# Router logits summed in PSUM on two quarters of the array's columns, in place of four partial rows and summing products

## The chip, the cores and the metric

One core of a Trainium2 chip runs the whole program. The metric is device time in microseconds for one execution; the table below has the median of three runs of the kernel before. Engines are called by their names here and by the profile's short names in the rows: TensorE (PE, its weight loads PEld), VectorE (DVE), ScalarE (ACT), GpSimd (POOL), SyncE (SP, its queue SPq).

## The reference

Two parts follow each other. A retention layer (4 batches, 8 heads, 768 tokens, 64 wide) gives rows x of 512 elements for 3072 tokens. A mixture of 8 experts then sends every token to the expert whose embedding has the largest logit:

```python
xn = x / (np.linalg.norm(x, axis=-1, keepdims=True) + 1e-06)
en = expert_emb / (np.linalg.norm(expert_emb, axis=-1, keepdims=True) + 1e-06)
logits = xn @ en.T / tau
expert_idx = np.argmax(logits, axis=1)
probs = np.exp(logits - logits.max(-1, keepdims=True))
gate_w = (probs / (probs.sum(-1, keepdims=True) + 1e-09))[np.arange(N), expert_idx]
out[mask] = gate_w[mask, None] * (np.maximum(x[mask] @ w1[e], 0.0) @ w2[e])   # for each expert e
```

The change concerns `x @ en.T`, the logits before the row norm, and what is made of them: the difference to the largest one and the choice of the expert.

## The kernel before, in words

The program is one written-out order of instructions for each engine; no scheduler moves them. It has two stages.

**Retention with routing (up to about 112 us).** Twelve blocks `m` of 256 tokens each go through a loop. For a block TensorE does, in this order: the scores of the 256 tokens (`scores`, L398), the products of queries with the state (`inter`, L466), the state of the next block (`state`, L433), the logits of the block before (`logits_products`, L515), four runs of four transposes that turn the keys and queries of the next block (L367, L385), and the products of values with masked scores (`intra`, L466 again). PSUM tiles for scores, logits and turned blocks come from four banks in rotation (`pt_`), so a run of transposes takes the bank that an earlier step of the same block had, once VectorE or ScalarE has read it. Blocks 0 to 2 get their logits only in block 3, all three at once, since the normed expert embedding `enT` is not ready sooner.

The 512 elements of a row lie as four row blocks of 128 in `yTs[m]` (128 partitions x 4 x 256 tokens). `logits_products` makes one product of 256 tokens for each of the four row blocks: its weights are `enT[:, j]` (128 x 32, of which 8 columns are experts), and the four products write the four different quarters of PSUM's partitions, that is of the array's columns. They are partial sums. `logits_rows` (L523) turns them on VectorE, 32 x 32 at a time, to `parts`, with tokens on the partitions. For a group of blocks (`GROUPS`: blocks 0-2, 3-5, 6-7, 8, 9-10, 11) `sums` (L533) then adds the four partial sums by four products with a 0/1 matrix (`quarters`), which also puts four sets of 32 tokens onto the 128 partitions. `choose` (L541 on) takes the maximum and the difference, finds the expert, `add_counts` counts, and in the next block `count` (L563 on, TensorE) and `ranks` give every token its place in its expert's table, to which GpSimd writes it (`place`, L599).

Rows of x go to memory by SyncE's queue (`rows`, L502), after VectorE has turned them (`rows_turn`, L495). From block 8 on SyncE also loads the weights of the experts (L211 to L220). Loads and rows that stand late in that queue carry a dependence on the early gather of tokens for expert 0 (L628).

**Experts (from about 114 us).** For each expert TensorE makes 96 products of the first layer (L265) and 96 or more of the second (L1117, L1163) from operands that are split into a high and a low part; VectorE makes the low part of the weights (L243) and of the hidden layer (L271). Two tiles of high and low columns, `xh`/`xl` and `hh`/`hl`, are views made by `columns` (L1091) with a distance between planes given by `PITCH` (L45).

Of the kernel before, what the change touches and what calls it, by code (L numbers as in the profile page):

```python
# [11 lines left out]
F32 = mybir.dt.float32  # L12
F32R = mybir.dt.float32r
# [4 lines left out]
ALU = mybir.AluOpType  # L18
AX = mybir.AxisListType
# [5 lines left out]
P = 128  # L25
B, H, S, D = 4, 8, 768, 64
T2 = 2 * P
# [14 lines left out]
CAP = max(CAPS)  # L42
NXC = -(-CAP // Q)
CAPW = NXC * Q
PITCH = [CAP if c % P == 0 else c if e == NE - 2 else CAPW for e, c in enumerate(CAPS)]  # L45
OV = 352
EARLY = 280
TURNED = [c % P > 0 and e < NE - 1 for e, c in enumerate(CAPS)]
# [61 lines left out]
def retention_moe(ctx: ExitStack, tc: tile.TileContext, q, k, v, emb, tau, w1, w2, const, const16, out):  # L110
# [401 lines left out]
    def logits_products(m, ps=None):  # L512
        ps = pt_() if ps is None else ps
        for j in range(KT):
            nc.tensor.matmul(ps[j * Q:(j + 1) * Q, :T2], enT[:, j, :], yTs[m][:, j, :], start=True, stop=True,  # L515
                             skip_group_check=True)
        return ps

    def logits_rows(m, ps):
        g = group_of[m]  # L520
        if g not in parts:
            parts[g] = ap_.tile([P, max(map(len, GROUPS)), 2, NQ, Q], F32, name="parts")
        nc.vector.transpose(out=parts[g][:, m - GROUPS[g][0]].rearrange("p u g e -> p (u g) e"),  # L523
                            in_=ps[:, :T2].rearrange("p (g b) -> p g b", b=Q))

    def span(g):
        return slice(2 * GROUPS[g][0], 2 * GROUPS[g][-1] + 2)
# [1 line left out]
    def sums(g, ps=None, fresh=False, room=None):  # L529
        nm = len(GROUPS[g])  # L530
        ps = pt_() if ps is None else ps
        for i in range(NQ):
            nc.tensor.matmul(ps[i * Q:(i + 1) * Q, :2 * nm * NE], C("quarters"),  # L533
                             parts[g][:, :nm, :, i, :NE].rearrange("p m u e -> p (m u) e"), start=not fresh, stop=True,
                             skip_group_check=True)
        at = room if fresh else ps[:, 64:]
        return [a[:, :2 * nm * NE].rearrange("p (n e) -> p n e", e=NE) for a in (ps, at)] + [at[:, 48:48 + NE]]

    chosen = []

    def choose(g, zs):  # L541
        z, w, _ = zs
        r = span(g)
        nb = r.stop - r.start
        bc = lambda t: t.unsqueeze(2).broadcast_to([P, nb, NE])
        m = ap_.tile([P, nb], F32, name="m", bufs=1)
        nc.vector.tensor_reduce(out=m, in_=z, axis=AX.X, op=ALU.max)
        yield
        nc.vector.tensor_tensor(out=z, in0=z, in1=bc(m), op=ALU.subtract)
        yield  # L550
        nc.vector.scalar_tensor_tensor(out=w, in0=z, scalar=0.0,
                                       in1=C("e16").unsqueeze(1).broadcast_to([P, nb, NE]), op0=ALU.is_lt, op1=ALU.add)
        yield
        nc.vector.tensor_reduce(out=wmn[:, r], in_=w, axis=AX.X, op=ALU.min)
        yield
        chosen.append(nc.vector.tensor_tensor(out=oh[:, r], in0=w, in1=bc(wmn[:, r]), op=ALU.is_equal))
        yield
# [253 lines left out]
    for m in range(NM):  # L811
# [57 lines left out]
        else:  # L869
# [28 lines left out]
            if m == 2:  # L898
                after(nc.sync.dma_start(
                    out=tbl.rearrange("(e s) c -> e (s c)", e=NE)[:, :FILL * SW].rearrange("e (p x) -> e p x", p=P // NE),  # L900
                    in_=none), i)
            for i in () if m < 3 else (0, 1, 2) if m == 3 else (m - 1,):
                logits_rows(i, logits_products(i))
            if m == NM - 5:
                pad(0, spare(0, 3), True)
# [4 lines left out]
            if nxt:  # L910
                state_sums(m + 1)
                if m == NM - 2:
                    lows[0]()
                transpose_k(m + 1, 0)
                transpose_q(m + 1, 0)
                i = transpose_q(m + 1, 1)
                if m + 3 < NM:
                    after(load_v(m + 3), i)
                transpose_k(m + 1, 1)
                if done is not None:  # L920
                    z = sums(done, spare(0, done % 3), True, spare(0, 3))
                    run_all(choose(done, z))
                    run_all(add_counts(done, z))
                if m == NM - 2:
                    lows[1]()
                if m == NM - 2:
                    load_piece(gathered)
                    load_piece(gathered)
                rows(m - 1, gathered if m == NM - 2 else None)
                intra(m, 0)  # L930
                intra(m, 1)
            else:
                intra(m, 0)
                take(m, 0)
                rows_turn(m - 1, (0,))
                z = sums(done)
                run_all(choose(done, z))
                run_all(add_counts(done, z))
                rows_turn(m - 1, (1,))
                rows(m - 1, x=xs_[m - 1])  # L940
                intra(m, 1)
# [146 lines left out]

    xts = {}

    def columns(name, k, e):  # L1091
        t = hp.tile([P, k, CAPW], F32R, name=name)
        return t.rearrange("p k c -> p (k c)")[:, :k * PITCH[e]].rearrange("p (k c) -> p k c", k=k)

    def x_turn(e, kt):
        if kt == 0:
            xTs[e] = (columns("xh", KT, e), columns("xl", KT, e))
        xt = xts[e, kt] = mp.tile([P, NXC, Q], F32, name="xt", bufs=2)
        n = blocks_of(e)
        nc.vector.transpose(out=xt[:, :n], in_=xgs[e][:, :n, kt * Q:(kt + 1) * Q])  # L1100
# [176 lines left out]
    for e in range(1, NE):  # L1277
        nxt = e + 1 < NE
        c = CAPS[e]
        cols = slice(0, c)  # L1280
        hh, hl = columns("hh", FT, e), columns("hl", FT, e)
        gsteps = iter(())
        last = None
        for ft in range(FT):
# [166 lines left out]
```

## Time and profile before

| what | value |
|---|---|
| median of 3 runs | 396.85 us (396.44 to 399.21) |
| the profiled execution | 396.12 us |
| its span, first to last instruction | 394.3 us |
| granted TensorE clock over the span | 1.000 |
| TensorE busy | 384.3 us, 97% |
| VectorE, ScalarE, GpSimd busy | 252.6, 214.6, 154.8 us |

The span is the time from the first to the last instruction of one profiled execution; its own time of 396.12 us has 1.8 us around the span. Times inside the span count from its start. "Busy" is time in which at least one instruction of the engine or the group runs, so a group of overlapping products has less busy time than its count times its mean. The chain is followed back from the last instruction, at each step to what released it.

### The profile page before, as it was taken

What the parts mean: (1) busy time and instruction counts of PE and PEld (TensorE: products, weight loads), DVE (VectorE), ACT (ScalarE), POOL (GpSimd) and SP (SyncE); (2) the same over time, 40 slices, a digit from 0 to 9 for tenths busy, and PEclk for the clock granted to TensorE, in tenths of its full rate; (3) what the DMA queues carried; (4) which work ended last, traced back from release to release, by engine and by line L of the source; (5) the groups of instructions that cost most, each with busy time, mean ns of one, the idle gap of its engine ahead of it and who ended that gap; (6) DMA issues with size and microseconds to landing.
All of it is one profiled execution on the core that took longest, in us unless ns stands there. A gap on an engine that the chain in (4) does not pass through costs nothing.

```text
span 394.3 us, 9699 instructions
## 1 busy us (share of the span) xinstructions
PE 384.3 (97%) x3714; PEld 359.4 (91%) x3714; DVE 252.6 (64%) x536; ACT 214.6 (54%) x383; POOL 154.8 (39%) x177
## 2 busy tenths in 40 slices
PE   7999999988999999999999999999999999999995
PEld 3899888877879898999999999999889999999985
DVE  5496876977988648853871874667357756476500
ACT  3585566655876175526553843935675534573411
POOL 2856397585844614203802510530282131121032
PEclk9999999999999999999999999999999999999999
DMA  7898999689469787976778796886979676675121
GB/s 237 260 305 256 268 267 281 180 240 262 98 197 288 237 249 217 298 183 225 251 244 215 257 333 184 256 282 204 264 259 347 191 230 227 169 240 158 30 107 56
DMA packets 91029, 89.20 MB, mean 226 GB/s; under 512 B 10796, under 2 KB 69548, under 8 KB 90972
## 3 DMA queue, kind: packets, MB, share of 16 engines
q1 hardware_dynamic: 85916, 75.39, 64.1%
q0 software_dynamic: 4880, 13.03, 9.2%
q8 instruction: 31, 0.51, 0.6%
q14 instruction: 26, 0.21, 0.2%
q10 hardware_dynamic: 176, 0.07, 0.1%
HBM read 65.00 MB, written 18.79 MB: 212 GB/s over the span
## 4 chain that ended last, share of the span: by engine, by line
PE 77%; DMA 13%; DVE 4%; issue 2%; SPq 1%; POOL 1%; POOLq 0%; ACT 0%; DVEq 0%
DMA out_dram<-og,si 10%; PE b L265 10%; PE pst L1117 9%; PE py L466 9%; PE py L265 8%; PE py L1117 7%; PE pst L265 6%; PE b L398 6%; PE b L1117 4%; PE pst L433 3%; PE pst L1163 3%; PE b L367 3%; PE b L385 2%; PE b L515 2%; PE pst L1203 2%
## 5 line engine op out<-in xcount | busy, mean ns | idle before, releaser
L243 DVE TENSOR_TENSOR wlo<-raw,whi 128x1024 fp32r<-128x1024 f32 x64 | 77.6, 1217 | 15.9 <-ACT whi L239 12.9
L1144 POOL DMA_INDIRECT out_dram<-og,si x26 | 27.0, 1039 | 115.0 <-ACT og L1134 65.2
L239 ACT CAST whi<-raw 128x1024 fp32r<-128x1024 f32 x64 | 66.1, 1044 | 1.3 <-DMA raw<-in_moe_w_dram 1.2
L628 POOL DMA_INDIRECT xr<-xd,gi x24 | 29.3, 1220 | 29.5 <-ACT sq L297 14.9
L265 PE MATMUL b<-xh,whi 128*128 128x360 f32 (+5 forms) x104 | 34.3, 334 | 0.0
L265 PE MATMUL b<-xl,whi 128*128 128x360 f32 (+5 forms) x104 | 34.1, 332 | 0.0
L265 PE MATMUL b<-xh,wlo 128*128 128x360 f32 (+5 forms) x104 | 34.0, 332 | 0.0
L419 DVE TENSOR_TENSOR pm<-b,mask 128x512 f32<-128x512 f32 x48 | 29.8, 683 | 4.8 <-PE b L398 4.5
L1100 DVE STREAM_TRANSPOSE xt<-xg 128x384 f32<-128x384 f32 (+1 forms) x28 | 15.6, 578 | 25.4 <-DMA xg<-xs 25.3
L270 ACT ACTIVATE hh<-b 128x360 fp32r<-128x360 f32 (+5 forms) x26 | 12.6, 484 | 34.9 <-PE b L265 34.9
L356 POOL TENSOR_TENSOR hh<-whi,cst 128x512 f32<-128x512 f32 x22 | 23.1, 1068 | 19.5 <-DVE pm L419 14.3
L599 POOL DMA_INDIRECT tbl<-zt,sloti x24 | 25.4, 1060 | 12.6 <-DVE sloti L590 3.5
L1117 PE MATMUL pst<-hh,wlo 128*128 128x360 f32 (+4 forms) x88 | 29.4, 334 | 0.8 <-DVE wlo L243 0.8
L1117 PE MATMUL pst<-hl,whi 128*128 128x360 f32 (+4 forms) x88 | 29.4, 334 | 0.0
L1117 PE MATMUL pst<-hh,whi 128*128 128x360 f32 (+4 forms) x88 | 29.3, 332 | 0.0
L265 PE MATMUL py<-xl,whi 128*128 128x384 f32 (+5 forms) x84 | 27.7, 334 | 0.0
L265 PE MATMUL py<-xh,whi 128*128 128x384 f32 (+5 forms) x84 | 27.5, 333 | 0.0
L265 PE MATMUL py<-xh,wlo 128*128 128x384 f32 (+5 forms) x84 | 27.2, 330 | 0.0
L361 POOL TENSOR_TENSOR hl<-wlo,cst 128x512 f32<-128x512 f32 x22 | 22.8, 1052 | 10.0 <-DMA wlo<-in_k_dram 8.3
L466 PE MATMUL py<-pm,vs 128*64 128x128 f32 x384 | 24.4, 277 | 1.0 <-issue 1.0
L398 PE MATMUL b<-qT,kT 64*128 64x128 f32 x384 | 24.7, 278 | 0.0
L466 PEld LDWEIGHTS py<-pm,vs 128*64 128x64 f32 x384 | 21.0, 137 | 3.0 <-issue 1.7
(237 smaller groups left out, 1026.0 us busy)
## 6 DMA issues: line engine op xcount, KB each, us to landing
raw<-in_moe_w_dram SPq DMA_DIRECT2D x60, 512.0 KB, 4.7
whi<-in_q_dram SPq DMA_DIRECT2D x24, 256.0 KB, 4.0
xd<-x SPq DMA_DIRECT2D x48, 128.0 KB, 6.3
wlo<-in_k_dram SPq DMA_DIRECT2D x11, 512.0 KB, 6.1
xs<-xr SPq DMA_DIRECT2D x6, 768.0 KB
og<-yt SPq DMA_DIRECT2D x72, 48.0 KB, 3.1
whi<-in_v_dram SPq DMA_DIRECT2D x6, 512.0 KB
wlo<-in_v_dram SPq DMA_DIRECT2D x6, 512.0 KB
```

The source lines that it names most:

```text
L239: nc.scalar.copy(out=views[1], in_=views[0])
L243: nc.vector.tensor_tensor(out=views[2], in0=views[0], in1=views[1].bitcast(F32), op=ALU.subtract)
L265: nc.tensor.matmul(acc[:, :w], a, x[:, kt, cols], start=(n == 0), stop=(n == len(todo) - 1))
L356: return eng.tensor_tensor(out=qs_r[:, m % 3, :, a], in0=qin[m % 3][:, a], in1=w, op=ALU.mult)
L361: return eng.tensor_tensor(out=ks_r[:, m % 3, s, h], in0=kin[m % 3][:, h, s], in1=w[:, h], op=ALU.mult)
L398: nc.tensor.matmul(psc[a][:, j], kTs[m][a * D:(a + 1) * D, j, u].rearrange("p s c -> p (s c)"), q_cols(m, a, j, u), start=True, stop=True, ...
L419: o.append(nc.vector.tensor_tensor(out=pm, in0=psc[a], in1=w, op=ALU.mult))
L466: nc.tensor.matmul(pys[m][u][o * D:(o + 1) * D, j], lhsT, rhs, start=first, stop=True, skip_group_check=True)
L599: i = nc.gpsimd.indirect_dma_start(out=tbl[:, :], out_offset=bass.IndirectOffsetOnAxis(ap=sloti[:, n:n + 1], axis=0), in_=zt[:, n], in_off ...
L628: return nc.gpsimd.indirect_dma_start(out=xr[:n, j, :], out_offset=None, in_=xd[:rows_, :], in_offset=bass.IndirectOffsetOnAxis(ap=gi[:n, ...
L1117: nc.tensor.matmul(acc[:, :c], a[:, f], x[:, kt, :c], start=(n == 0), stop=(n == 3 * FT - 1))
L1144: i = nc.gpsimd.indirect_dma_start(out=out[:, :] if h is None else out.rearrange("t (h x) -> (t h) x", h=2), out_offset=bass.IndirectOffse ...
```

## The change

The logits of a block are summed over the four row blocks in PSUM, by accumulation. The 256 tokens of a block are split into two sets of 128 (`y[:, i::2]`), and each set is accumulated over the four row blocks on a quarter of its own, the first two of the array's columns. A block has eight products of 128 tokens in place of four of 256. VectorE turns the result in two parts of 64 x 64 to `parts`, where the 256 tokens already stand on 128 partitions in two columns. `sums` makes no products any more and only names PSUM space for what follows; `choose` reads the logits from `parts` and puts the maximum into PSUM. The logits of blocks 1 and 2 move behind later transposes of block 3. The planes of the expert tiles get another distance.

```diff
-PITCH = [CAP if c % P == 0 else c if e == NE - 2 else CAPW for e, c in enumerate(CAPS)]
+PITCH = [CAP if c % P == 0 else CAPW for c in CAPS]
     def logits_products(m, ps=None):
         ps = pt_() if ps is None else ps
         for j in range(KT):
-            nc.tensor.matmul(ps[j * Q:(j + 1) * Q, :T2], enT[:, j, :], yTs[m][:, j, :], start=True, stop=True,
-                             skip_group_check=True)
+            y = yTs[m][:, j].rearrange("p (u g b) -> p g u b", u=2, b=Q)
+            for i in range(2):
+                nc.tensor.matmul(ps[i * Q:(i + 1) * Q, :P].rearrange("p (h u b) -> p h u b", h=2, b=Q), enT[:, j, :], y[:, i::2],
+                                 start=(j == 0), stop=(j == KT - 1), skip_group_check=True)
         return ps

     def logits_rows(m, ps):
...
-            parts[g] = ap_.tile([P, max(map(len, GROUPS)), 2, NQ, Q], F32, name="parts")
-        nc.vector.transpose(out=parts[g][:, m - GROUPS[g][0]].rearrange("p u g e -> p (u g) e"),
-                            in_=ps[:, :T2].rearrange("p (g b) -> p g b", b=Q))
+            parts[g] = ap_.tile([P, max(map(len, GROUPS)), 2, Q], F32, name="parts")
+        for h in range(2):
+            nc.vector.transpose(out=parts[g][2 * h * Q:2 * (h + 1) * Q, m - GROUPS[g][0]],
+                                in_=ps[:2 * Q, 2 * h * Q:2 * (h + 1) * Q].rearrange("p (u b) -> p u b", b=Q))

     def sums(g, ps=None, fresh=False, room=None):
         nm = len(GROUPS[g])
         ps = pt_() if ps is None else ps
-        for i in range(NQ):
-            nc.tensor.matmul(ps[i * Q:(i + 1) * Q, :2 * nm * NE], C("quarters"),
-                             parts[g][:, :nm, :, i, :NE].rearrange("p m u e -> p (m u) e"), start=not fresh, stop=True,
-                             skip_group_check=True)
...
     def choose(g, zs):
-        z, w, _ = zs
+        z, w, _, m = zs
...
-        m = ap_.tile([P, nb], F32, name="m", bufs=1)
-        nc.vector.tensor_reduce(out=m, in_=z, axis=AX.X, op=ALU.max)
+        s = parts[g][:, :nb // 2, :, :NE].rearrange("p m u e -> p (m u) e")
+        nc.vector.tensor_reduce(out=m, in_=s, axis=AX.X, op=ALU.max)
         yield
-        nc.vector.tensor_tensor(out=z, in0=z, in1=bc(m), op=ALU.subtract)
+        nc.vector.tensor_tensor(out=z, in0=s, in1=bc(m), op=ALU.subtract)
...
-            for i in () if m < 3 else (0, 1, 2) if m == 3 else (m - 1,):
+            if m > 2:
+                i = 0 if m == 3 else m - 1
                 logits_rows(i, logits_products(i))
...
                 transpose_q(m + 1, 0)
+                if m == 3:
+                    logits_rows(1, logits_products(1))
                 i = transpose_q(m + 1, 1)
...
                 transpose_k(m + 1, 1)
+                if m == 3:
+                    logits_rows(2, logits_products(2))
...
-        hh, hl = columns("hh", FT, e), columns("hl", FT, e)
+        hh = hp.tile([P, FT, CAPW], F32R, name="hh")
+        hl = hp.tile([P, FT, CAPW], F32R, name="hl")
```

TensorE in block 3, before: the logits of blocks 0 to 2 (tiles b_777, b_784, b_790, four products each), the four runs of transposes, the summing products of the first group (`pst_591<-parts`), and the first product of `intra`.

```order
L515 MATMUL b_777<-yT,enT 32x256 x4
L515 MATMUL b_784<-yT,enT 32x256 x4
L515 MATMUL b_790<-yT,enT 32x256 x4
L367 MATMUL b_800<-ident,hl 128x128 x4
L385 MATMUL b_808<-ident,hh 128x128 x4
L385 MATMUL b_814<-ident,hh 128x128 x4
L367 MATMUL b_821<-ident,hl 128x128 x4
L533 MATMUL pst_591<-parts,cst_61 32x48 x4
L466 MATMUL py_698<-pm_710,vs 64x128
```

The same place after: the logits of block 0 (b_777), 1 (b_807) and 2 (b_831), eight products of 128 tokens each.

```order
L517 MATMUL b_777<-yT,enT 32x128 x8
L367 MATMUL b_793<-ident,hl 128x128 x4
L385 MATMUL b_801<-ident,hh 128x128 x4
L517 MATMUL b_807<-yT,enT 32x128 x8
L385 MATMUL b_818<-ident,hh 128x128 x4
L367 MATMUL b_825<-ident,hl 128x128 x4
L517 MATMUL b_831<-yT,enT 32x128 x8
L466 MATMUL py_698<-pm_710,vs 64x128
```

The three sets of logits stand apart, the last one right ahead of `intra`, and the summing products are gone. In the other blocks the logits keep their place ahead of the transposes.

VectorE in block 3, before: it turns the three sets of logits, makes the state sums (`s`), and begins the choice of the first group.

```order
L523 STREAM_TRANSPOSE parts<-b_777 128x256
L523 STREAM_TRANSPOSE parts<-b_784 128x256
L523 STREAM_TRANSPOSE parts<-b_790 128x256
L446 TENSOR_TENSOR s_796<-pst_591,tB 128x256
L451 TENSOR_TENSOR s_798<-pst_591,tB 128x256
L547 TENSOR_REDUCE m<-pst_591 128x6
L549 TENSOR_TENSOR pst_591<-pst_591,m 128x48
```

The same place after.

```order
L526 STREAM_TRANSPOSE parts<-b_777 64x64 x2
L446 TENSOR_TENSOR s_789<-pst_591,tB 128x256
L451 TENSOR_TENSOR s_791<-pst_591,tB 128x256
L526 STREAM_TRANSPOSE parts<-b_807 64x64 x2
L526 STREAM_TRANSPOSE parts<-b_831 64x64 x2
L546 TENSOR_REDUCE pst_591<-parts 128x6
L548 TENSOR_TENSOR pst_591<-parts,pst_591 128x48
```

The state sums now stand ahead of the second and third set, and the maximum and the difference read `parts` itself.

## Rows read from the trace of the kernel before

**Rows 1.** The page: busy time, share of the span, instructions of TensorE.

```profile
PE 384.3 (97%) x3714; PEld 359.4 (91%) x3714; DVE 252.6 (64%) x536; ACT 214.6 (54%) x383; POOL 154.8 (39%) x177
```

**Rows 2.** Stages: start:end, length, busy (count) PE PEld DVE ACT POOL, clock, DMA, GB/s.

```profile
9.00:63.00 54.00, 54.00 (x1119) 48.27 (x1118) 38.96 (x86) 35.66 (x65) 34.17 (x35) 1.00 0.92 272
94.00:112.00 18.00, 18.00 (x325) 15.75 (x323) 16.18 (x41) 14.97 (x24) 14.15 (x18) 1.00 0.55 142
112.00:134.00 22.00, 21.20 (x181) 19.19 (x178) 19.02 (x57) 12.30 (x25) 10.57 (x11) 1.00 0.79 227
160.00:293.00 133.00, 133.00 (x719) 129.77 (x718) 81.30 (x148) 71.54 (x126) 40.27 (x40) 1.00 0.79 243
390.00:394.30 4.30, 0.00 (x0) 0.00 (x0) 0.00 (x0) 0.24 (x1) 0.97 (x1) 1.00 0.10 35
```

**Rows 3.** Waits of TensorE: total us, times, longest.

```profile
PE pst L433 <- issue: 1.2, 1, 1.2
PE py L466 <- issue: 1.0, 1, 1.0
PE pst L1117 <- DVE wlo L243: 0.8, 2, 0.4
```

**Rows 4.** The chain: start us, us, what; logits, transposes and sums.

```profile
38.71 1.43 PE b L515 x24
40.14 0.59 PE b L367 x4
...
41.60 0.44 PE b L367 x4
42.04 0.22 PE pst L533 x8
...
48.36 0.57 PE b L515 x8
```

**Rows 5.** Instructions of L515 and L523 (ns min/median/max), and who waits for L533.

```profile
L515 PE MATMUL b<-yT,enT x96: 379/379/403, 38.6 to 114.3; 128*32 128x256 f32 x96
...
L523 DVE STREAM_TRANSPOSE parts<-b x12: 437/449/450, 39.3 to 114.8; 128x256 f32<-128x256 f32 x12
...
  DVE m L547: 4.6, 6
```

**Rows 6.** The chain: products on two places (x16, x32 of intra), on four (inter).

```profile
42.26 1.90 PE py L466 x32
...
46.41 1.03 PE py L466 x32
...
110.15 1.02 PE py L466 x16
```

**Rows 7.** VectorE in order of time: the maximum of the first group.

```profile
42.33 0.21 DVE L547 TENSOR_REDUCE m<-pst 128x6 f32<-128x48 f32 x1 [1.03 <-PE pst L533]
```

**Rows 8.** Block 5 in order of time, and the lines' row of L495.

```profile
57.31 0.45 DVE L523 STREAM_TRANSPOSE parts<-b 128x256 f32<-128x256 f32 x1 [0.98 <-PE b L515]
...
58.43 0.47 PEld L367 LDWEIGHTS b<-ident,hl 128*128 128x128 f32 x4
...
L495 DVE STREAM_TRANSPOSE x<-yT 128x512 f32<-128x512 f32 x24 | 15.6, 686 | 0.9 <-DMA xd<-x 0.9
```

**Rows 9.** The chain from 101 to 132 us, and a wait of SyncE's queue.

```profile
101.25 0.92 PE pst L433 x32
...
123.00 0.67 DVE x L495
...
132.10 0.89 PE pst L1117 x4
...
SPq L211 <- DMA xge<-xd,gi: 5.7, 1, 5.7
```

**Rows 10.** The chain: 24 first-layer products of experts 5 and 6.

```profile
304.92 3.93 PE b L265 x24
...
324.60 3.94 PE b L265 x24
```

More of the change, by code (lines that the diff above doesn't have):

```diff
@@ L531, in sums @@
         ps = pt_() if ps is None else ps
-        for i in range(NQ):
-            nc.tensor.matmul(ps[i * Q:(i + 1) * Q, :2 * nm * NE], C("quarters"),
-                             parts[g][:, :nm, :, i, :NE].rearrange("p m u e -> p (m u) e"), start=not fresh, stop=True,
-                             skip_group_check=True)
         at = room if fresh else ps[:, 64:]
-        return [a[:, :2 * nm * NE].rearrange("p (n e) -> p n e", e=NE) for a in (ps, at)] + [at[:, 48:48 + NE]]
+        return [a[:, :2 * nm * NE].rearrange("p (n e) -> p n e", e=NE) for a in (ps, at)] + [at[:, 48:48 + NE], at[:, 56:56 + 2 * nm]]
     chosen = []
     def choose(g, zs):
-        z, w, _ = zs
+        z, w, _, m = zs
         r = span(g)
@@ L1089, in retention_moe, with columns @@
     xts = {}
-    def columns(name, k, e):
-        t = hp.tile([P, k, CAPW], F32R, name=name)
-        return t.rearrange("p k c -> p (k c)")[:, :k * PITCH[e]].rearrange("p (k c) -> p k c", k=k)
+    def columns(name, e):
+        t = hp.tile([P, KT, CAPW], F32R, name=name)
+        return t.rearrange("p k c -> p (k c)")[:, :KT * PITCH[e]].rearrange("p (k c) -> p k c", k=KT)
     def x_turn(e, kt):
         if kt == 0:
-            xTs[e] = (columns("xh", KT, e), columns("xl", KT, e))
+            xTs[e] = (columns("xh", e), columns("xl", e))
         xt = xts[e, kt] = mp.tile([P, NXC, Q], F32, name="xt", bufs=2)
```

## The prediction

> **What bounds the kernel now.** I read the summary first [rows 1]: TensorE is busy for 384.3 of the 394.3 us of the span. The stages come second [rows 2]: from 9 to 63 us and from 94 to 112 us TensorE has no idle time at all, and none from 160 to 293 us; the span ends 4.3 us after its last work. The granted clock is 1.00 in each of them, so no part of the time is to be put down to the clock. The waits of TensorE come third [rows 3]: it waits 0.8 us in two places for a low half of the weights from VectorE, and stops twice, for 1.2 and 1.0 us, for nothing that the profile shows. So work added to TensorE in the retention stage (up to 112 us) goes to the end of the run, unless one of these few stops swallows it. Work added to or taken from VectorE, ScalarE and the queues counts only where TensorE waits for it.
>
> The rows of the chain tell what the logits cost TensorE today [rows 4]. The three blocks whose logits are made together (24 instructions, since each product is issued as two) take 1.43 us; a block on its own (8 instructions) takes 0.57 us, and there are nine of those. Sixteen instructions more cost 0.86 us, which is 54 ns each, and 0.14 us is left as a fixed part. One such instruction lasts 379 ns in the records [rows 5], so several run at a time: the four products of a block write four different quarters of the array's columns. The summing products of a group (8 instructions) take 0.22 us.
>
> **The products, part by part.** After the change a block has eight products of 128 columns, 16 instructions, and they use two quarters of the columns only. The columns that pass are as many as before, spread over half the places. The trace has a near relative: the products of values and masked scores inside a block (128 columns, K of 128, two halves of the columns in turn, also two instructions each). 16 of them take 1.02 us and 32 take 1.90 us [rows 6], which is 55 ns for each further one and 0.14 us fixed. I take 1.02 us for a block. That is 0.45 us more than now, for nine blocks 4.05 us. For the three blocks it is 3 x 1.02 - 1.43 = 1.63 us. There the products now stand apart, between transposes (the order of TensorE is in the section on the change): a run of four transposes that follows the logits takes 0.59 us and a later one 0.44 us [rows 4], so one more such passage adds 0.15 us. Sum of what is added: 5.83 us.
>
> The bounds of this term: products on four places at a time (the products of queries and state, 32 in 1.03 us) would make 16 take 0.52 us; products with no overlap at all, such as the full transposes at 0.11 us each (four in 0.44), would make them take 1.76 us. The first would be 0.05 us less for a block than now, the second 1.19 us more. I take the middle one because it has the same K, the same number of columns and the same two places in turn.
>
> The Trainium skill (TensorEngine Tiling (Array Packing), Theoretical Speedup and When to Use Tiling) speaks against this change: a stationary side of at most 32 columns lets four column tiles work, with up to four times the speed, and two tiles are half of that. The trace agrees in kind, since 256 columns in 379 ns end every 54 ns. Taken to the letter it doubles the whole 0.57 us, which is the fourth rival below; by it the sum would be 1.4 us higher.
>
> **The sums.** Six groups lose four products each (8 instructions). At 0.22 us each this takes 1.3 us off TensorE. VectorE loses its wait for them, 4.6 us over six groups (1.03 us in the first, [rows 5, 7]); this wait goes, but nothing on TensorE hung on it in the retention stage. The maximum, the difference and the rest of the choice stay the same number of VectorE instructions; the first two read the transposed logits in SBUF, and the maximum is now written to PSUM. I cost that at nothing: each lasts about 0.2 us, VectorE has idle time in each of these stretches [rows 2], and the counting products that need the choice come a whole intra stage (1.90 us) later. In the block after the third, the chain of choice now begins only after the last product of logits. From there two transposes (0.4 to 0.9 us, below) and five operations of 0.21 us [rows 7] need 1.5 to 2.0 us, so the choice arrives as the counting starts; at worst it costs 0.1 us once.
>
> **VectorE's transposes.** Twelve of 128x256 (0.449 us, [rows 5]) become twenty-four of 64x64. The trace shows none of that size. The nearest rows are 0.2 us (a reduction of 48 columns, [rows 7]) and 0.45 us, so a block costs 0.4 to 0.9 us. Who waits for them: the second half of the key transposes takes the bank that the logits had. Today the transpose ends at 57.76 us and TensorE takes the bank at 58.43 [rows 8], 0.67 us later. Even at 0.9 us that leaves 0.2 us. I cost it at nothing; if each lasted over 0.56 us, TensorE would wait in nearly every block.
>
> **The stretch from 112 to 134 us** is where some of the extra goes missing. TensorE's 0.8 us of waits stand here [rows 2, 3]. Followed back on the chain [rows 9], the low half that it waits for ends VectorE work that runs without a break from 123.0 us, and that began when a write of x had landed (VectorE's one wait of 0.9 us, last of [rows 8]). That write sits in SyncE's queue behind loads that waited 5.7 us for the early gather, and the gather hangs on TensorE's state products at about 102 us. So this chain moves later by what is added up to 102 us only. After that TensorE gets three blocks of logits (3 x 0.45) and loses two sums (0.44): 0.9 us more of its own. It will therefore meet the low half with hardly any wait left. I take 0.7 of the 0.8 us as swallowed.
>
> **The columns' pitch.** The expert tiles get another distance between planes (360 or 408 become 408 or 416). No instruction changes its shape. The trace already has both ends: 24 first-layer products of 360 columns take 3.93 us at pitch 416 (expert 5) and 3.94 us at pitch 360 (expert 6) [rows 10]. The planes of the hidden layer are read in the same way, so I take the same for them: nothing, within 0.01 us for 24 products.
>
> **Sum.** 5.83 - 1.3 - 0.7 = 3.8 us. The profiled execution took 396.12 us around its span of 394.3 us, and would take 399.9 us. The median of the runs before is 396.85 us, 0.7 us above it, so the forecast is 400.7 us.
>
> **Rivals.**
> First, the two unexplained stops (1.16 and 1.00 us, [rows 3]) end at a time of their own. By then TensorE is 3.4 us later (1.63 + 0.15 + 5 x 0.45 - 3 x 0.22), so both could vanish: 3.8 - 2.2 = 1.6 us, 398.5 us. For it: the runs before spread from 396.44 to 399.21. Against it: nothing in the profile released TensorE there, so the stops may well move along.
> Second, and on the other side, the two places overlap as four do: 16 instructions in 0.52 us. Then it is 9 x (-0.05) + 3 x 0.52 - 1.43 + 0.15 - 1.3 = -1.5 us, 395.4 us, a little faster. The point from which it decides: below 0.70 us a block the sum is negative. Against it stands the row of 1.02 us, which has the same two places.
> Third, no overlap: 9 x 1.19 + 3 x 1.76 - 1.43 + 0.15 - 1.3 - 0.8 = 12.6 us, 409.5 us. For it only that weights of a quarter might not load beside a product of the same quarter; against it, the same row.
> Fourth, the fixed part doubles as well: 1.14 us a block, 9 x 0.57 + 1.99 + 0.15 - 1.3 - 0.8 = 5.2 us, 402.0 us.
> Fifth, the bank: if a 64x64 transpose took as long as a 128x512 one (0.69 us, the last of [rows 8]), two end 0.26 us after TensorE wants the bank, in eleven blocks 2.9 us more: 403.6 us.
>
> **How the numbers follow.** Forecast 0.60, with its own range of 399.4 to 402.0 us; first rival 0.12, second 0.07, third 0.04, fourth 0.13, fifth 0.04. The range of 398.0 to 403.3 us takes in the forecast, the first and the fourth, and leaves out most of the second, third and fifth. A measurement of this kernel can tell about 1% from no change, which is 4.0 us. The forecast stands just inside it (+3.8), so its 0.60 is split, 0.32 within and 0.28 above. Slower by over 1%: 0.28 + 0.13 + 0.04 + 0.04 = 0.49. Within 1%: 0.32 + 0.12 and nearly half of the second, 0.47. Faster by over 1%: what remains of the second if still other waits go with it, 0.04.
>
> **What would show it.** Right: a block's logits at about 1.0 us on the chain where they now have 0.57, a span some 3.8 us longer of which 3 lie before 102 us, hardly a wait of TensorE for a low half at 136 us, and stages of the experts of the same length. Wrong: logits at 0.5 to 0.6 us a block (then faster), at 1.7 (then far slower), key transposes that wait for the logits' transposes, or stops for nothing visible that are more or fewer than two.

## The result, and the profile after

The changed kernel takes 402.74 us (median, 401.62 to 404.09), the kernel before 397.59 us beside it: a ratio of 1.0127, interval 1.0098 to 1.0155, so 5.0 us slower. The profiled execution took 402.03 us around a span of 400.1 us. Times are compared among executions within 1.5% of their kernel's fastest; one execution of one experiment (409.07 us) lies outside and is left out of its time.

The page of the changed kernel answers to [rows 1]; TensorE has 48 instructions more and 6.5 us more busy time.

```profile
PE 390.8 (98%) x3762; PEld 366.2 (92%) x3762; DVE 253.7 (63%) x548; ACT 215.1 (54%) x383; POOL 154.1 (39%) x177
```

The chain (start us, us, what) answers to [rows 4]: a block's logits, 16 instructions, take 1.00 us where they had 0.57, and in block 3 they stand between transposes.

```profile
38.19 1.00 PE b L517 x16
39.19 0.59 PE b L367 x4
...
40.21 1.00 PE b L517 x16
...
42.23 1.00 PE b L517 x16
43.23 1.90 PE py L466 x32
...
49.33 1.00 PE b L517 x16
```

The instructions of VectorE's new transposes (ns min/median/max) answer to the second row of [rows 5]; two of them last about as long as the one before.

```profile
L526 DVE STREAM_TRANSPOSE parts<-b x24: 231/243/245, 39.2 to 120.9; 64x64 f32<-64x64 f32 x24
```

The stages (start:end, length, busy of PE, PEld, DVE, ACT, POOL, clock, DMA, GB/s) answer to [rows 2]. The clock is 1.00 in each, so the time is not the clock's. TensorE has 0.33 us idle from 112 to 138 us, where it had 0.80 from 112 to 134. New are 1.75 us from 94 to 112 us, and 0.11 us in the stage of the experts, which had none.

```profile
9.00:63.00 54.00, 54.00 (x1117) 49.05 (x1115) 38.39 (x89) 33.92 (x61) 33.52 (x34) 1.00 0.88 259
94.00:112.00 18.00, 16.25 (x267) 13.98 (x257) 13.86 (x37) 10.94 (x18) 13.18 (x15) 1.00 0.60 154
112.00:138.00 26.00, 25.67 (x269) 23.35 (x266) 22.80 (x65) 16.86 (x33) 8.88 (x12) 1.00 0.61 175
164.00:297.00 133.00, 132.89 (x718) 129.50 (x717) 83.17 (x151) 73.76 (x129) 40.51 (x40) 1.00 0.80 249
```

TensorE's waits (total us, times, longest) answer to [rows 3]. The two stops of over 1 us are gone; five shorter ones stand in blocks 6, 9 and 10, and one at the x of expert 1.

```profile
PE b L398 <- ACT kT L372: 0.9, 2, 0.5
PE py L466 <- issue: 0.6, 2, 0.3
PE py L466 <- ACT yT L486: 0.5, 1, 0.5
...
PE b L265 <- DVE xl L1111: 0.3, 1, 0.3
```

The price of the products is as forecast. Open after this trace were 1.2 us that the sum lacked, and whether the waits of the last blocks belong to the change.

### The profile page after: what moved, and what is told of

It is laid out like the page before. It is cut to its first block, busy times and chain, and to the rows that moved or that the text cites. A ratio compares the mean times of both kernels' runs of the same rounds, so it can differ in the third digit from the quotient of the medians.

```text
span 400.1 us, 9815 instructions
## 1 busy us (share of the span) xinstructions
PE 390.8 (98%) x3762; PEld 366.2 (92%) x3762; DVE 253.7 (63%) x548; ACT 215.1 (54%) x383; POOL 154.1 (39%) x177
## 4 chain that ended last, share of the span: by engine, by line
PE 60%; DMA 16%; issue 7%; DVE 6%; SPq 6%; POOL 2%; ACT 2%; POOLq 0%; DVEq 0%; ACTq 0%
DMA out_dram<-og,si 10%; PE py L466 8%; PE b L265 6%; PE pst L1121 6%; PE b L398 6%; PE py L265 6%; PE pst L265 4%; PE py L1121 4%; SPq L1133 4%; PE b L517 3%; PE pst L433 3%; PE b L367 3%; PE pst L1167 3%; PE b L385 2%; DVE wlo L243 2%
## 5 line engine op out<-in xcount | busy, mean ns | idle before, releaser
L243 DVE TENSOR_TENSOR wlo<-raw,whi 128x1024 fp32r<-128x1024 f32 x64 | 77.7, 1217 | 17.6 <-ACT whi L239 12.0
L627 POOL DMA_INDIRECT xr<-xd,gi x24 | 29.5, 1230 | 35.4 <-ACT sq L297 18.2
L265 PE MATMUL b<-xl,whi 128*128 128x360 f32 (+5 forms) x104 | 34.4, 335 | 0.3 <-DVE xl L1111 0.3
L265 PE MATMUL b<-xh,wlo 128*128 128x360 f32 (+5 forms) x104 | 34.2, 334 | 0.1
L265 PE MATMUL b<-xh,whi 128*128 128x360 f32 (+5 forms) x104 | 34.3, 334 | 0.0
L265 PE MATMUL py<-xl,whi 128*128 128x384 f32 (+5 forms) x84 | 28.0, 335 | 0.0
L265 PE MATMUL py<-xh,whi 128*128 128x384 f32 (+5 forms) x84 | 27.5, 333 | 0.0
L265 PE MATMUL py<-xh,wlo 128*128 128x384 f32 (+5 forms) x84 | 27.2, 330 | 0.0
L398 PEld LDWEIGHTS b<-qT,kT 64*128 64x128 f32 x384 | 22.4, 188 | 2.3 <-ACT kT L372 1.3
```

The lines of the kernel that those rows point to most:

```text
L243: nc.vector.tensor_tensor(out=views[2], in0=views[0], in1=views[1].bitcast(F32), op=ALU.subtract)
L265: nc.tensor.matmul(acc[:, :w], a, x[:, kt, cols], start=(n == 0), stop=(n == len(todo) - 1))
L398: nc.tensor.matmul(psc[a][:, j], kTs[m][a * D:(a + 1) * D, j, u].rearrange("p s c -> p (s c)"), q_cols(m, a, j, u), start=True, stop=True, ...
L627: return nc.gpsimd.indirect_dma_start(out=xr[:n, j, :], out_offset=None, in_=xd[:rows_, :], in_offset=bass.IndirectOffsetOnAxis(ap=gi[:n, ...
```

## The experiments

Each is compared with the kernel before on its own chip: 396.54 us for the first four, 394.19 for the next four, 394.72 for the last four.

**Both kernels again, for their traces.** Unchanged.

> The kernel before, once more, for a second trace. Theory A (the stops of TensorE in the retention stage that nothing visible releases are scatter): the two stops of 1.0 and 1.2 us stand elsewhere, or are of another number, while a block of the loop without a stop still lasts 8.31 to 8.33 us and the logits of a block 0.57 us. Theory B (they belong to the program): they stand at the same instructions with the same length, about 2.2 us in all.

> The changed kernel, once more, for a second trace. Theory A (stops are scatter): logits 1.00 us a block and 8.74 us for a block of the loop without a stop, as in the first trace, but the late copies of ScalarE in blocks 9 and 10 (2.1 us lost in block 10) stand elsewhere or are gone. Theory B (the change makes them): block 10 lasts 10.8 us again because a copy of the turned keys comes late again.

Measured: 397.69 and 403.02 us. The kernel before now shows no stop of 1 us; the changed one shows its late waits in blocks 9 and 10 again. The stops belong to the execution. The late waits stayed open here.

**Four quarters, 64 tokens each.**

```diff
-            for i in range(2):
-                nc.tensor.matmul(ps[i * Q:(i + 1) * Q, :P].rearrange("p (h u b) -> p h u b", h=2, b=Q), enT[:, j, :], y[:, i::2],
+            for i in range(NQ):
+                nc.tensor.matmul(ps[i * Q:(i + 1) * Q, :2 * Q].rearrange("p (u b) -> p u b", b=Q), enT[:, j, :], y[:, i],
...
-        for h in range(2):
-            nc.vector.transpose(out=parts[g][2 * h * Q:2 * (h + 1) * Q, m - GROUPS[g][0]],
-                                in_=ps[:2 * Q, 2 * h * Q:2 * (h + 1) * Q].rearrange("p (u b) -> p u b", b=Q))
+        nc.vector.transpose(out=parts[g][:, m - GROUPS[g][0]], in_=ps[:, :2 * Q].rearrange("p (u b) -> p u b", b=Q))
```

> Logits still summed in PSUM and no summing products, but on all four quarters of the columns, 64 tokens each: 16 products of 64 columns, 32 instructions a block, and one transpose of 128x64. Theory A (two places in place of four are what costs): the columns pass as fast as before the change; at 14.5 ns an instruction, the rate of the state products of 64 columns on four places, 32 take 0.46 us and with the fixed 0.14 us 0.60 us a block, against 0.57 before and 1.00 after. With three sets apart (3 x 0.60 - 1.43 + 0.15), nine blocks (9 x 0.03) and the sums gone (-1.3) it is -0.4 us against the kernel before, so 0.997 to 1.001 of it, and 4.5 to 5 us below the changed kernel. Theory B (the number of products and weight loads costs): 32 instructions at the 55 ns of a two-place product make 1.8 us a block, and the kernel is 13 us slower than before.

Measured: 405.85 us (402.68 to 407.03), ratio 1.0189, interval 1.0148 to 1.0229. That is 7.5 us slower, where theory A has 0.4 us faster and theory B 13 us slower. The first row is from its chain, the next four from TensorE's waits, the last from its stages.

```profile
49.65 0.58 PE b L517 x32
```

```profile
PE b L367 <- issue: 2.6, 2, 2.2
PE b L367 <- DVE parts L525: 2.1, 1, 2.1
PE py L265 <- DVE xl L651: 1.9, 1, 1.9
...
PE b L517 <- issue: 1.2, 2, 0.6
```

```profile
126.00:130.00 4.00, 4.00 (x23) 3.84 (x21) 3.48 (x10) 0.41 (x1) 2.99 (x3) 0.57 0.36 91
```

The product's part of the theory holds: on four places a block costs 0.58 us again, with twice the instructions, and a block without sums lasts 8.32 us as before. So the 0.43 us are the price of two places, not of more instructions. The end did not follow: 7.8 us of waits stand in these four rows, and a granted clock of 0.57 over 4 us (mostly the lower of its levels, 1.2 GHz), right after the wait of 1.9 us, adds its own loss, as does one of 0.64 over the 4 us after the wait of 2.2 us. The two waits of over 2 us stand in blocks 9 and 10, where ScalarE copies the keys 3.5 to 3.6 us after their transposes; the other traces on this chip have late key copies as well (last section), so the form need not be their cause. Why the others came is open.

**The changed kernel with the summing products back** (nothing reads what they write; the choice still takes the logits themselves).

```diff
+        for i in range(NQ):
+            nc.tensor.matmul(ps[i * Q:(i + 1) * Q, :2 * nm * NE], C("quarters"),
+                             parts[g][:, :nm, :, :NE].rearrange("p m u e -> p (m u) e"), start=not fresh, stop=True,
+                             skip_group_check=True)
```

> The changed kernel with the four summing products of each group put back as work whose output is overwritten unread (they multiply the finished logits by the 0/1 matrix). Theory A (the sums are worth their time on TensorE): 6 x 0.22 = 1.3 us slower than the changed kernel, ratio to the kernel before about 1.016. Theory B (nothing hung on them, they fit into waits): within 0.3 us of the changed kernel, ratio about 1.0127.

Measured: 402.91 us (402.46 to 403.54), ratio 1.0156, interval 1.0122 to 1.0191. Against the one execution of the changed kernel on that chip (403.02 us) this is no loss, as theory B has it; against that kernel's ratio of 1.0127 it is 1.1 us more, as theory A has it. It doesn't tell the two apart. The products put back also bring a wait of their own: in block 3 TensorE stands 0.6 us for VectorE's turn of the logits, and the block takes 12.03 us instead of 11.14.

**The logits' products twice, in the kernel before.** The work is repeated, nothing is left out.

```diff
-        for j in range(KT):
+        for j in 2 * list(range(KT)):
```

> The kernel before, with each block's logits products issued a second time on the same four quarters; the summing products stay. A block then has 16 product instructions, as many as in the changed kernel, on four places instead of two. Both theories give 0.14 + 16 x 0.054 = 1.00 us a block (0.43 more) and 24 x 0.054 = 1.3 us more for the three blocks together. Theory A (what the changed kernel loses beyond the sum of its steps, 1 to 2 us in blocks 6, 9 and 10 and at the second expert, follows from TensorE being some 4 to 5 us late with that many small products, in whatever form): 9 x 0.43 + 1.3 = 5.2 us more, 402 to 403.5 us, ScalarE's key copies late by over 0.5 us in block 9 or 10, a wait for the x of expert 1 or 2. Theory B (it belongs to the new form, two places and the two transposes): no late key copies, the wait of 0.8 us swallowed and not given back, 4.4 us or less more, 401 to 402 us.

Measured: 399.90 us (398.36 to 401.73), ratio 1.0131, interval 1.0096 to 1.0166: 5.2 us slower, like the changed kernel, though its places, transposes and sums are those of before. The key copies are on time in all blocks (0.1 to 0.3 us after their transposes). The profiled execution has a stop for nothing visible of 1.6 us, and at expert 2 (TensorE in order of time):

```profile
197.68 0.45 PE L265 MATMUL b<-xh,wlo 128*128 128x400 f32 x1 [0.69 <-DVE wlo L243]
```

Theory A is right on the time and on a wait that comes with any such lateness, here for the low weights of expert 2. It is wrong on the key copies, and so is theory B that ties the wait to the new form.

**The logits of blocks 0 to 2 together again.**

```diff
-            if m > 2:
-                i = 0 if m == 3 else m - 1
+            for i in () if m < 3 else (0, 1, 2) if m == 3 else (m - 1,):
...
-                if m == 3:
-                    logits_rows(1, logits_products(1))
...
-                if m == 3:
-                    logits_rows(2, logits_products(2))
```

> The changed kernel, with the logits of blocks 0 to 2 made together in block 3 as in the kernel before. Theory A (one more passage between transposes costs a fixed 0.15 us, and the second passage of logits as much again): block 3 is 0.2 to 0.3 us shorter than the changed kernel's (10.85 instead of 11.14 us) and the end 0.2 us earlier, which the time can't tell. Theory B (the standing apart is what makes room for VectorE; together, the second half of the key transposes waits for VectorE's six small transposes): block 3 no shorter or longer by 0.2 to 0.5 us.

Measured: 399.05 us (398.07 to 399.72), ratio 1.0108, interval 1.0079 to 1.0137. Block 3 lasts 10.74 us instead of 11.14. Standing apart costs 0.4 us, somewhat over theory A.

**The new form in blocks 0 to 8 alone, and in blocks 9 to 11 alone.** A set of groups decides between the two forms.

```diff
+    NEWG = (0, 1, 2, 3)
...
+            if group_of[m] not in NEWG:
+                nc.tensor.matmul(ps[j * Q:(j + 1) * Q, :T2], enT[:, j, :], yTs[m][:, j, :], start=True, stop=True,
+                                 skip_group_check=True)
+                continue
```

> The changed kernel, with the logits of blocks 9 to 11 made in the old way (four quarters, 256 tokens, summing products); blocks 0 to 8 in the new way. Steps alone: block 3 1.5 us more and 6 x 0.43 = 2.6 us, 4.1 us before the swallowed wait. Theory A (the excess comes from the new form where it stands in blocks 9 to 11, beside the last gathers and loads): it goes, the blocks from 3 to 11 take 71 + 4.1 = 75 us instead of 76.8, and the end is at +3.3 us, 400.5 to 401.2 us. Theory B (it comes from being late there, in whatever form): blocks 9 and 10 stay at 9.9 to 10.9 us, +4.2 to +5 us, 401.8 to 402.6 us.

> The reverse: blocks 0 to 8 in the old way, the logits of blocks 9 to 11 in the new way. Steps alone: 3 x 0.43 = 1.3 us less two sums (0.44). Theory A (the new form itself makes the signals late in the last blocks): 1 to 2 us on top, 2 to 3 us more in all, 399.5 to 400.6 us, with late key copies in block 10. Theory B (the lateness of the whole stage makes them): 0.5 to 1.3 us more, 398.1 to 398.9 us, partly swallowed by the wait for the low half.

Measured: 400.28 us (399.67 to 401.81), ratio 1.0148, interval 1.0117 to 1.0178, for the early one; 394.60 us (393.26 to 397.37), ratio 1.0019, interval 0.9995 to 1.0044, for the late one. For the late blocks the steps say 0.86 us (3 x 0.43 less two sums); the time says 0.75 us, between -0.2 and 1.7, which can't tell that from nothing. In its trace expert 0's second layer starts 0.82 us later, counted from the first block, than in the third trace of before (below), and expert 1 starts 0.01 us later: the stretch between, with TensorE's wait for the low half, took all of it, where theory B has a part. The early blocks cost all of the loss (5.8 us, between 4.6 and 7.0), and blocks 9 and 10 were not long there (8.90, 8.33 us). Their trace pays at two places where no new product stands: 1.41 us of wait for the early gather, and 1.28 us from expert 1 to expert 3's second layer. So the loss is not made by the form of the last blocks, nor in them, which neither theory had.

**Both kernels once more, on one chip, and the old pitch.** The third run is the changed kernel with the distances of before.

```diff
-PITCH = [CAP if c % P == 0 else CAPW for c in CAPS]
+PITCH = [CAP if c % P == 0 else c if e == NE - 2 else CAPW for e, c in enumerate(CAPS)]
...
-        hh = hp.tile([P, FT, CAPW], F32R, name="hh")
-        hl = hp.tile([P, FT, CAPW], F32R, name="hl")
+        hh, hl = columns("hh", FT, e), columns("hl", FT, e)
```

> The kernel before as it is, for its trace beside the other runs of this chip. Theory A (stops for nothing visible and late key copies belong to single executions): clean blocks of 8.3 us, key copies of ScalarE late by 0.1 us after their transposes or late in other blocks than in the first two traces. Theory B (they belong to the kernel): 1.0 to 1.7 us of stops in blocks 8 to 10 again.

> The changed kernel as it is, beside its own kernel before. Theory A (the steps' sum, with nothing swallowed in the end: clean blocks +0.43, block 3 +1.5, so 9 x 0.43 + 1.5 less what the sums gave, 4.5 to 5.4 us at the end; the 1 to 2 us of late key copies in blocks 9 and 10 come and go): +4.5 to +5.4 us, blocks 4 to 10 at 8.74 to 9.3 us if no copy is late. Theory B (blocks 9 and 10 are always long in the changed kernel): 1 to 2 us in those blocks again.

> The changed kernel with the old distances between planes of the expert tiles. Theory A (a plane's distance costs nothing): the time of the changed kernel within 0.5 us, each expert's layers of the same length to 0.02 us. Theory B (the new distance is worth up to a microsecond either way): a difference of over 0.5 us in the stages of experts 5 and 6 and no other.

Measured: 394.10 us for the kernel before; 399.27 us (398.71 to 403.28), ratio 1.0101, interval 1.0066 to 1.0136, for the changed one; 399.63 us (398.71 to 401.94), ratio 1.0108, interval 1.0072 to 1.0144, with the old pitch. The pitch is worth nothing that the times can tell; in the traces the stretch from expert 3's second layer to the last product takes 147.02 us in the eight with the new distance and 147.10 us in the six with the old one. The profiled execution of the changed kernel is its 403.28 us, with two stops of the kind seen before. Blocks 9 and 10 take 8.91 and 8.75 us in it, so theory B, by which they are always long, falls. The one with the old pitch has no stops and no late key copies, so it stands for the changed kernel in what follows. Its execution is the slowest of its four: the first block starts 0.88 us later than in the third trace of before, and the end after the last product lasts 1.74 us longer.

**TensorE alone late.** The kernel before, with two sets of first-layer products of expert 0 repeated after the routing's last step.

```diff
             acc = acc_()
+            if ft > FT - 3:
+                for _ in first_layer(0, ft, acc, xh0, xl0, early):
+                    pass
             yield from first_layer(0, ft, acc, xh0, xl0, early, {0: (0, 2, 1), 4: (0, 1, 2)}.get(ft))
```

> The kernel before, with two sets of 12 first-layer products of expert 0 issued twice (24 x 0.128 = 3.07 us of TensorE alone), after the last choice and count of the routing, so that TensorE is late and the chain of tables, gathers and x of experts 1 and 2 is not. Theory A (the changed kernel swallowed 0.8 to 1.0 us at 112 to 134 us and gave it back at experts 1 and 2, because that chain is as late there as TensorE): here the 0.8 us wait for the low half goes and nothing is given back, so 2.1 to 2.5 us more at the end, no wait for the x or the low weights of experts 1 and 2. Theory B (the late stretches at experts 1 and 2 come with any lateness of TensorE, as the loads of weights go by its pace): 3.0 us or more, a wait of 0.3 to 0.7 us at expert 1 or 2.

Measured: 395.37 us (394.42 to 398.64), ratio 1.0021, interval 0.9997 to 1.0045. Of 3.07 us added, 0.8 reach the end (-0.1 to 1.8 by the interval; 0.84 in the traces, from the first block to the last product). Theory A had the direction and the place, but not the size, since 2.2 us are covered. The chain of the kernel before on the same chip shows by what:

```profile
119.52 5.42 DMA tbl<-zt,sloti
...
124.95 1.61 DMA tb<-tbl
...
127.44 1.13 DVE wlo L243
128.57 0.36 DVE hl L271
128.93 1.14 DVE wlo L243
...
130.11 0.89 PE pst L1117 x4
```

and the chain with the repeated products, that it is TensorE's own work without a gap (the second layer is L1120 here):

```profile
125.18 3.06 PE pst L265 x24
128.25 3.07 PE pst L1120 x24
```

TensorE's waits of before on that chip put the low halves at 1.3 us:

```profile
PE pst L1117 <- DVE wlo L243: 1.3, 2, 0.8
```

The price, read from the starts of rows, is 2.2 us: expert 0's second layer and what follows to expert 1 took 27.37 us before and 25.14 with TensorE late.

## Why the prediction was right and wrong

The time of 402.74 us lies in the stated range of 398.0 to 403.3 us, but above the forecast's own range of 399.4 to 402.0. The loss of 5.0 us against 3.8 is closer than the steps were: in the table below two steps are short by 2.4 us and three are too high by 0.95 us, and that these cancel in part is luck.

The third trace of before and the one with the old pitch have no stops and no late copies, so they can be set side by side. Up to block 3 they are alike (25.52 us). Times are differences of starts of TensorE's rows. The table rests on this one pair; what lies ahead of the first block and behind the last product, 0.88 and 1.74 us more in the changed one, is not in it.

| stage | before | changed | more | forecast |
|---|---|---|---|---|
| block 3 | 9.65 | 11.14 | 1.49 | 1.56 |
| blocks 4 to 10 | 59.86 | 61.84 | 1.98 | 2.49 |
| block 11 to expert 0's second layer | 21.81 | 23.31 | 1.50 | 0.46 |
| from there to expert 1 | 27.37 | 26.30 | -1.07 | -0.7 |
| expert 1, expert 2, first layer of expert 3 | 87.48 | 88.85 | 1.37 | 0 |
| the rest | 147.09 | 147.09 | 0 | 0 |
| sum | | | 5.27 | 3.8 |

**The products: right.** 1.00 us a block against 1.02; blocks without a sum grew from 8.31 to 8.74 us, 0.43 against 0.45. The Trainium skill (TensorEngine Tiling (Array Packing), Theoretical Speedup) allows up to four times the speed for a side of at most 32 and up to twice for one of at most 64. The traces agree for all but the fixed part: less 0.14 us, a block takes 0.86 us on two places and 0.44 on four.

**Block 3, the transposes and the pitch: right.** 1.49 us against 1.56, of which 0.4 us is the standing apart (0.43 in the forecast: two more fixed parts of 0.14 us and 0.15 us for a passage). Two 64x64 transposes take 0.49 us of VectorE against 0.4 to 0.9, and the key transposes never waited for them in the clean trace. The pitch gives back 0.08 us in all.

**The sums: right where they stand, open at the end.** Blocks 6, 8 and 9, which lose a sum, grew by 0.20, 0.24 and -0.18 us instead of 0.43: the sums gave 0.23, 0.19 and 0.61 us where 0.22 was forecast. The third is more because TensorE had waited for VectorE ahead of that sum, which the forecast had left out (third trace of before, TensorE in order of time):

```profile
93.16 0.26 PE L533 MATMUL pst<-parts,cst 128*32 128x16 f32 x8 [0.24 <-DVE s L451]
```

So block 9 lasts 9.09 us before and 8.91 changed, although it has 0.43 us more of products. What the sums are worth at the end stays open.

**The step that failed: "the stretch from 112 to 134 us is where some of the extra goes missing".** The step took a chain beside TensorE to move by the lateness up to 102 us only and TensorE to move further, so that 0.7 us of wait would be swallowed for good. The wait did shrink (-1.07 us). But the premise was wrong in both directions, and with it one of the prediction's own signs, stages of the experts of the same length.

The chain itself was read without one of its rows. In the trace of [rows 9] the first of the writes of x waits 0.5 us in SyncE's queue until VectorE has turned the logits of block 11, so it hangs on TensorE's last logits too, and not only on what was added up to 102 us:

```profile
114.93 0.36 DVE parts L523
115.29 0.13 SPq L502
```

Ahead of it, TensorE turns the rows that the early gather brings. In the kernel before the gather is just in time; GpSimd issues its last part at 106.74 us and TensorE starts at 109.57 (GpSimd and TensorE in order of time, third trace of before):

```profile
102.07 0.33 POOL L622 TENSOR_SCALAR gi<-tb 128x1 int32<-128x1 f32 x1
...
106.74 1.04 POOL L628 DMA_INDIRECT xge<-xd,gi  x1 [0.31 <-POOL gi L622]
...
109.57 0.87 PE L647 MATMUL pst<-ident,xge 128*128 128x128 f32 x6
```

and changed:

```profile
105.98 0.96 POOL L621 TENSOR_SCALAR gi<-tb 128x1 int32<-128x1 f32 x1
...
111.29 0.21 POOL L621 TENSOR_SCALAR gi<-tb 24x1 int32<-24x1 f32 x1 [0.61 <-DMA tb<-tbl]
112.31 1.05 POOL L627 DMA_INDIRECT xge<-xd,gi  x1 [0.80 <-POOL gi L621]
...
113.98 0.44 PE L646 MATMUL pst<-ident,xge 128*128 128x128 f32 x2
115.70 0.55 PE L646 MATMUL pst<-ident,xge 128*128 128x128 f32 x3 [1.28 <-DMA xge<-xd,gi]
```

Counted from the first block (8.70 us in the one, 9.57 in the other), the last issue moved by 4.70 us and TensorE's first need by 3.54. From its first index (`gi`) to the last issue GpSimd took 4.67 us before and 6.33 changed; 0.61 us of that is a wait for the last piece of the table to be read, and that read started 3.8 us after the last table write ahead of it was issued, 2.5 us before the change. Why the table came later wasn't tried. So 1.28 us of wait is new where the forecast had the two lost sums as a gain. The same wait is 1.25 us in the third trace of the changed kernel, 1.03 us with the three blocks together and 1.41 us with the early blocks alone. It isn't in the first two traces of the changed kernel, where late key copies held TensorE up ahead of it.

Behind it, the x of experts 1 and 2 hang on the last table writes, and these on the last choice. Counted from the first block, the last write was issued 4.77 us later (at 119.52 and 125.16 us), about as far as the whole retention stage moved (4.97 us up to expert 0's second layer). It also took longer to land, so the table was read 6.1 us later (before at 124.95, in the chain above; changed, SyncE in order of time):

```profile
131.96 0.35 SPq L1028 DMA_DIRECT2D tb<-tbl  x1
```

TensorE began expert 1 only 3.90 us later, since it had saved 1.07 us, and so came too early to expert 2. In the chain of the changed kernel (old pitch) the work of ScalarE and VectorE runs ahead of TensorE there:

```profile
182.12 1.96 DMA og<-yt
...
184.86 0.70 ACT og L1138
...
187.25 1.05 ACT whi L239
188.33 1.23 DVE wlo L243
...
194.76 1.23 DVE wlo L243
...
196.48 2.19 PE py L265 x12
```

where the chain of before has TensorE's products alone (`PE b L265 x12` at 188.50, then `PE py L265 x12` at 190.69). VectorE's first turn of expert 2's x waits longer for the rows, but it is done 5 us before the low half that needs it. That one waits for ScalarE's copy of x (`xh`), and ScalarE stands until then at expert 0's output rows (`og`), which come by SyncE's queue, behind the rows of expert 2 (VectorE and ScalarE in order of time, before and then changed):

```profile
174.35 1.10 DVE L1100 STREAM_TRANSPOSE xt<-xg 128x416 f32<-128x416 f32 x2 [2.39 <-DMA xg<-xs]
178.00 1.34 ACT L1134 ACTIVATE og<-og,gt 128x512 f32<-128x512 f32 x2 [6.66 <-DMA og<-yt]
181.16 0.57 DVE L1107 TENSOR_TENSOR xl<-xt,xh 128x400 fp32r<-128x400 f32 x1 [5.71 <-ACT xh L1101]
```

```profile
181.01 1.11 DVE L1104 STREAM_TRANSPOSE xt<-xg 128x416 f32<-128x416 f32 x2 [3.98 <-DMA xg<-xs]
184.23 1.34 ACT L1138 ACTIVATE og<-og,gt 128x512 f32<-128x512 f32 x2 [7.82 <-DMA og<-yt]
187.38 0.57 DVE L1111 TENSOR_TENSOR xl<-xt,xh 128x400 fp32r<-128x400 f32 x1 [5.27 <-ACT xh L1105]
```

Counted from the first block ScalarE starts on `og` 5.35 us later; TensorE's first product of expert 2 comes 4.20 us later. So ScalarE's lead, from its start on `og` to TensorE's first product of expert 2, shrinks from 10.3 to 9.2 us. In all fourteen traces the length of expert 2's first layer follows this lead:

| ScalarE's lead, us | 10.1 to 11.2 (six traces) | 9.8 | 9.5 | 9.5 | 9.2 | 9.0 | 8.8 | 8.6 | 8.4 |
|---|---|---|---|---|---|---|---|---|---|
| expert 2's first layer, us | 17.5 | 17.6 | 17.9 | 18.0 | 18.2 | 18.4 | 18.7 | 18.8 | 19.0 |

The time saved in between is not the whole reason. With the three blocks together and with the early blocks alone TensorE saved only 0.05 and 0.26 us, and expert 2's first layer still lost 0.52 and 1.18 us; there the table was read 5.2 and 5.7 us later than before, and expert 1 began 4.3 us later. What these traces have in common is that the chain of the tables moved further than TensorE. Why it did wasn't tried, and no run moved that chain alone. Of the 1.37 us, expert 2 has 0.73, expert 1 0.30 (its x is turned 2.75 us ahead of TensorE instead of 3.83) and expert 3 0.34, which was not followed.

The repeated products show the other side: TensorE alone was late there, the chain was not, and nothing was given back (87.48 us from expert 1 to expert 3's second layer in both).

So the forecast of +3.8 us was short by 1.04 us at the gather and 1.37 us at the experts, and 0.95 us too high in the blocks and the swallowed wait: 3.8 + 1.04 + 1.37 - 0.51 - 0.07 - 0.37 = 5.26.

**The rivals.** The first had half a case: stops for nothing visible come and go with the execution, in both kernels, so nothing ties them to the change. The second and third fall with 1.00 us a block. The fourth gave 402.0 us, close to the time, for a wrong reason: its fixed part didn't double. The fifth falls with 243 ns a transpose.

## What to carry to other kernels

Time added ahead of a point from which several chains start (here the routing: tables, gathers, x) moves the other side of a wait that stands behind it too, so such a wait can't be counted on: 1.07 us were covered in the changed kernel and 1.37 us came back at the experts, while with the late blocks alone all of 0.82 us was covered and nothing came back. Time added to one engine behind that point was covered for 2.2 of 3.07 us, and nothing came back. Before a wait is counted as swallowed, follow its other side back and ask whether it moves as far, and look for transfers that land just in time ahead of it. Read what a wait costs from the starts of the rows around it, not from the idle column.

## What the runs showed that was not expected

**Stops for nothing visible.** Those of the first trace of before [rows 3] are in neither later one. Two like them stand in the profiled execution of the changed kernel that took 403.28 us (TensorE in order of time):

```profile
62.72 1.97 PE L466 MATMUL py<-pm,vs 128*64 128x128 f32 x31 [1.14 <-issue]
...
69.24 0.46 PE L433 MATMUL pst<-wlo,hl 64*64 64x64 f32 x16 [0.85 <-issue]
```

In the DMA records a 16 KB transfer of instructions landed 1.4 us before each of these two ended (at 61.26 and 67.84 us), and so it did before the two of the first trace (85.41 and 91.80, stops to 86.78 and 93.17). The transfer before the first of each pair stood 11 us earlier. Six shorter or single stops in three other traces (0.45 to 1.63 us; the second trace of the changed kernel, the products twice, the four quarters) also end 1.2 to 1.5 us after such a transfer; the one before stood 10.6 and 9.5 us earlier in the first two of these traces, less than that on four quarters, and 9.8 us is also seen without a stop. The short stops in blocks 9 and 10 don't fit in. That TensorE lacked instructions is a reading, not shown.

**Late key copies.** In the first trace of the changed kernel ScalarE's copy of keys in block 10 began at 108.32 us, after an idle of 3.26 us, though TensorE's rows put the transposes that it waits for at 105.12 us (0.63 us). Usually it starts 0.1 us after them. Every trace on the chip of the first four experiments shows the like, the kernel before too (one copy 2.0 us late), and none on the two chips after. ScalarE in order of time:

```profile
108.32 0.59 ACT L372 COPY kT<-b 128x512 f32<-128x512 f32 x1 [3.26 <-PE b L367]
```

They put 1 to 2 us into blocks 9 and 10 of the changed kernel there. Their cause is open.
